# The last two output chunks: the second half stored chunk by chunk

## The chip, the cores and the metric

The kernel runs on one NeuronCore of a Trainium2 chip. The metric is the device time of one execution in microseconds (us), the median over several runs. A profiled execution of the same program gives, beside its time, a span: from the first to the last instruction on the core's engines. The engines are TensorE (PE in the profile, its weight loads PEld), VectorE (DVE), ScalarE (ACT), GpSimd (POOL) and SyncE (SP). SP, ACT and POOL each issue DMA transfers from a queue of their own (SPq, ACTq, POOLq); in the profile's DMA part, q1 carries SP's transfers, q10 ACT's and q0 POOL's.

## The reference: what is computed

The output is a sum over one array x of 2048 rows and 640 columns:

```python
xn = layernorm(x)
a, b = xn @ dft_hid_re.T, xn @ dft_hid_im.T          # along the 640 columns
fourier = dft_seq_re @ a - dft_seq_im @ b            # along the 2048 rows
mlp = gelu(xn @ w1 + b1) @ w2 + b2                   # 640 -> 1536 -> 640
out = x + fourier + mlp
```

All of it is float32. On the chip a float32 operand is split into a high and a low part, and a product is three matmuls (high-high, high-low, low-high).

## The kernel before, in words

The 2048 rows are taken in four row blocks of 512 (`NT = 4`, `TB = 512`). The first part of the kernel is the layernorm, the MLP and the products that build the transformed halves of the input; the last part, which starts long before the lines that matter here, runs the Fourier sums along the rows and then, for pairs of row blocks, the product with the hidden transform. What these leave in PSUM is transposed (the layout of the output in SBUF is 32-row bands, `B = 32`), added to the x + MLP part, and stored. The scheduling is by hand: each stage is a list of entries (`entries`), TensorE's matmuls of an entry are issued first, and `beside` or `hidden_beside` names what the other engines do behind that entry. The order in which the code names operations is the order in which they stand on each engine.

The change lies in the very last entries of the last pair. There, row block `ta` (tile `yo`, 128 partitions x 16 x 160 columns, `blocks[-2][1]`) still lacks its two last chunks of 32 columns in each 160-column quarter, columns 64 to 96 and 96 to 128, `2 * B : 4 * B`. They lie in the PSUM banks `X` and `X + 1`. In its last entries TensorE completes them in halves of 256 columns (`HALVES`), 15 matmuls each: the first half of bank `X`, the first half of bank `X + 1`, the second half of `X`, and last the second half of `X + 1`. Half `u` becomes the rows `u * 8` to `u * 8 + 8` of the 16 in `yo`. For each half:

- `turn_rows(u, j)` (L1703, its transpose is L1706) transposes half `u` of bank `X + j` on VectorE, into the scratch `rt2` or, with `dst`, straight into `yo`. For the very last one the old content of `yo` was added into the PSUM bank ahead, so that no add is left behind it.
- `add` (L462, its instruction is L463) adds the scratch into `yo`.
- `store_rows` (L1708) calls `store` (L1276, its DMA is L1280), which sends the rows to DRAM as one DMA for each of the four quarters, two from SP's queue and two from ACT's. With both chunks a run of 64 columns, 256 bytes, is contiguous; a DMA is 32 partitions x 8 rows x 256 bytes, 64 KB.

`upper_rows` does that for the first half, `lower_rows` for the second half: turn chunk 0, add it, turn chunk 1 into place, then four DMAs with both chunks. In front of them on the same queues stand the stores of the other row block of the pair (`out_dram<-u` on SP and ACT, `out_dram<-y` on POOL).

Every DMA of SP and ACT carries one of eight completion semaphores, which the framework gives out in turn in the order of issue over both queues. A DMA whose turn comes to a semaphore again waits, on its queue, until the DMA that had it before has landed. The closing code on SP (L1779) waits for the eight semaphores one after the other, in the fixed order of their numbers 0 to 7, and then all engines meet in two barriers. In the kernel before, the four DMAs of `upper_rows` have semaphores 1 and 3 (SP), 0 and 2 (ACT), and the four of `lower_rows` have 5 and 7 (SP), 4 and 6 (ACT).

Of the kernel before, what the change touches and what calls it, by code (L numbers as in the profile page):

```python
# [17 lines left out]
B = 32  # L18
# [8 lines left out]
def kernel(  # L27
# [45 lines left out]
    nc = tc.nc  # L73
# [18 lines left out]
    def pool(name, side="left", stack=ctx):  # L92
        return stack.enter_context(tc.tile_pool(name=name, bufs=1, side=side, reuse_waits="tile"))
# [22 lines left out]
    def bank(k):  # L116
        return banks[:, k]
# [19 lines left out]
    rows = pool("rows", side="right", stack=es_rows)  # L137
# [60 lines left out]
    def rows_of(ap, t):  # L198
        return ap[t * TB : (t + 1) * TB].rearrange("(n r) d -> r n d", r=B)
# [262 lines left out]
    def add(dst, a, b, op=ALU.add):  # L462
        nc.vector.tensor_tensor(dst, a, b, op=op)  # L463


    blocks = [(0, t) for t in range(NT)] + [(1, t) for t in (NT - 1, *range(NT - 1))]
# [239 lines left out]
    v, r, t = others[:, :, 1], others[:, :, 3], others[:, :, 4]  # L706
# [569 lines left out]
    def store(t, src, c0, c1, *queues, rows=slice(None)):  # L1276

        queues = queues or (nc.sync,)
        for q in range(Q):
            queues[q % len(queues)].dma_start(  # L1280
                rows_of(out, t)[:, rows, q * DQ + c0 : q * DQ + c1], src[q * B : (q + 1) * B]
            )
# [44 lines left out]
    yo = {}  # L1327
# [365 lines left out]
    def last_rows(u):  # L1693

        rows = slice(u * NB // 2, (u + 1) * NB // 2)
        return rows, yo[blocks[-2][1]][:, rows, 2 * B : 4 * B].rearrange("p n (e i) -> p e n i", i=B)

    def turned_rows(u):

        t = A["rt2"][:, 1, 0].rearrange("p a b -> p (a b)")[:, u * TB : (u + 1) * TB]  # L1700
        return t.rearrange("p (e n i) -> p e n i", e=2, i=B)

    def turn_rows(u, j, dst=None):  # L1703

        src = bank(X + j)[:, HALVES[u]].rearrange("p (n i) -> p n i", i=B)
        nc.vector.transpose(turned_rows(u)[:, j] if dst is None else dst, src)  # L1706

    def store_rows(rows):  # L1708

        t = blocks[-2][1]  # L1710
        store(t, yo[t][:, rows, 2 * B : 4 * B], 2 * B, 4 * B, nc.sync, nc.scalar, rows=rows)

    def upper_rows():

        rows, d = last_rows(0)
        add(d, d, turned_rows(0))
        store_rows(rows)

    def lower_rows():

        rows, d = last_rows(1)
        turn_rows(1, 0)
        add(d[:, 0], d[:, 0], turned_rows(1)[:, 0])
        turn_rows(1, 1, d[:, 1])
        store_rows(rows)

    first = 0
    for kind, what in stages:
# [55 lines left out]
```

## Time and profile before

| what | value |
|---|---|
| time, median of 3 runs | 850.54 us (850.37 to 850.61) |
| time of the profiled execution | 850.49 us |
| its span | 848.5 us |
| TensorE busy | 842.5 us, 99% of the span |
| VectorE busy | 687.1 us, 81% |
| ScalarE busy | 368.8 us, 43% |
| end of the last matmul | 844.44 us from the start of the span |
| end of the last VectorE instruction (L1706) | 844.92 us |

A row of the timeline has the start in us from the span's start, the duration, the engine, the line, the operation, output <- input and how many there are; a merged row covers several. The duration of a DMA row (SPq, ACTq) is the time that its queue takes to issue it, not that of the transfer; "to landing" is from the start of the issue to the last completion signal.

### The profile page before, as it was taken

How to read it: one execution, taken by the hardware profiler on the slowest of the kernel's cores; microseconds unless marked ns; L12 is line 12 of the kernel's file. 1: busy time of each engine (PE TensorE's matmuls, PEld its weight loads, DVE VectorE, ACT ScalarE, POOL GpSimd, SP SyncE). 2: the span in 40 equal slices, each digit the busy share in tenths (PEclk: the TensorE clock that was granted, in tenths of full speed). 3: DMA queues.
4: the chain of work that ended last, by engine and by line, in shares of the span. 5: the costliest groups of instructions: out<-in, count | busy, mean ns of one | idle time of the engine just before them, and what ended most of it. 6: DMA issues, size and time to landing. Idle time of an engine off the chain costs nothing.

```text
span 848.5 us, 10660 instructions
## 1 busy us (share of the span) xinstructions
PE 842.5 (99%) x3741; PEld 698.6 (82%) x3741; DVE 687.1 (81%) x912; ACT 368.8 (43%) x527; POOL 67.6 (8%) x116
## 2 busy tenths in 40 slices
PE   9999999999999999999999999999999999999998
PEld 7888888888888888888888888888888888888887
DVE  7969888767854778979979787899977998886687
ACT  7655666545453555443444343232322433223241
POOL 0440024222301000000000000000000000000002
PEclk9999999999999999999999999999999999999999
DMA  7995757878987897948744679663744799805354
GB/s 222 291 247 163 149 159 249 265 222 298 254 203 201 336 321 139 208 118 198 156 137 107 167 219 292 158 142 95 218 151 156 230 234 230 311 19 180 124 168 112
DMA packets 197094, 166.53 MB, mean 196 GB/s; under 512 B 59601, under 2 KB 168145, under 8 KB 196529
## 3 DMA queue, kind: packets, MB, share of 16 engines
q1 hardware_dynamic: 187296, 140.42, 61.8%
q0 software_dynamic: 7600, 24.91, 8.8%
q10 hardware_dynamic: 2144, 0.52, 0.3%
q8 instruction: 29, 0.48, 0.2%
q14 instruction: 25, 0.20, 0.1%
HBM read 115.75 MB, written 46.14 MB: 191 GB/s over the span
## 4 chain that ended last, share of the span: by engine, by line
PE 99%; DVE 0%; issue 0%
PE banks L301 30%; PE banks L300 30%; PE banks L302 30%; PE banks L320 10%; PE banks L666 1%; PE banks L682 0%; DVE zeros L655 0%; DVE yo L1706 0%; DVE warm L657 0%
## 5 line engine op out<-in xcount | busy, mean ns | idle before, releaser
L301 PE MATMUL banks<-as,xab 128*128 128x512 f32 (+1 forms) x417 | 160.1, 384 | 0.0
L300 PE MATMUL banks<-as,xab 128*128 128x512 f32 (+1 forms) x417 | 160.1, 384 | 0.0
L302 PE MATMUL banks<-as,xab 128*128 128x512 f32 (+1 forms) x417 | 160.1, 384 | 0.0
L186 ACT ACTIVATE as<-r 128x1024 fp32r<-128x1024 f32 x80 | 85.0, 1062 | 171.2 <-PE banks L302 147.4
L189 DVE TENSOR_TENSOR as<-r,as 128x1024 fp32r<-128x1024 f32 x80 | 97.1, 1215 | 38.1 <-ACT as L186 38.0
L301 PEld LDWEIGHTS banks<-as,xab 128*128 128x128 f32 x417 | 78.3, 188 | 15.6
L300 PEld LDWEIGHTS banks<-as,xab 128*128 128x128 f32 x417 | 78.3, 188 | 15.5
L302 PEld LDWEIGHTS banks<-as,xab 128*128 128x128 f32 x417 | 78.3, 188 | 15.4
L301 PE MATMUL banks<-as,xc 128*128 128x512 f32 x224 | 87.1, 389 | 0.0
L300 PE MATMUL banks<-as,xc 128*128 128x512 f32 x224 | 87.1, 389 | 0.0
L302 PE MATMUL banks<-as,xc 128*128 128x512 f32 x224 | 87.1, 389 | 0.0
L186 ACT ACTIVATE as<-rt 128x1024 fp32r<-128x1024 f32 x32 | 34.0, 1062 | 72.5 <-PE banks L302 57.9
L320 PE MATMUL banks<-xt,xab 128*128 128x512 f32 x240 | 56.8, 390 | 0.0
L189 DVE TENSOR_TENSOR hs<-ab,hs 128x512 fp32r<-128x512 f32 x36 | 24.7, 685 | 36.2 <-ACT hs L186 36.2
L320 PEld LDWEIGHTS banks<-xt,xab 128*128 128x128 f32 x240 | 45.0, 188 | 9.4
L301 PEld LDWEIGHTS banks<-as,xc 128*128 128x128 f32 x224 | 42.0, 188 | 8.8
L302 PEld LDWEIGHTS banks<-as,xc 128*128 128x128 f32 x224 | 42.0, 188 | 8.7
L300 PEld LDWEIGHTS banks<-as,xc 128*128 128x128 f32 x224 | 42.0, 188 | 8.7
L1280 POOL DMA_DIRECT2D out_dram<-u x4 | 2.6, 657 | 568.3 <-DVE u L463 568.3
L300 PE MATMUL banks<-hs,xc 128*128 128x512 f32 x120 | 46.7, 389 | 0.0
L301 PE MATMUL banks<-hs,xc 128*128 128x512 f32 x120 | 46.7, 389 | 0.0
L302 PE MATMUL banks<-hs,xc 128*128 128x512 f32 x120 | 46.7, 389 | 0.0
(240 smaller groups left out, 1679.8 us busy)
## 6 DMA issues: line engine op xcount, KB each, us to landing
raw<-in_A_dft_seq_re_dram SPq DMA_DIRECT2D x64, 256.0 KB, 5.4
raw<-in_A_dft_seq_im_dram SPq DMA_DIRECT2D x64, 256.0 KB, 5.1
w1r<-in_B_w_dram SPq DMA_DIRECT2D x144, 80.0 KB, 3.3
wit<-wst POOLq DMA_DIRECT2D x15, 384.0 KB, 4.3
wit<-wst POOLq DMA_DIRECT2D x20, 256.0 KB, 4.2
forms_ab<-xab SPq DMA_DIRECT2D x4, 1280.0 KB, 7.6
xab<-wit SPq DMA_DIRECT2D x13, 384.0 KB, 4.1
row<-xn SPq DMA_DIRECT2D x14, 320.0 KB, 5.3
```

The lines of the kernel that those rows point to most:

```text
L186: nc.scalar.activation(h, s, AF.Copy)
L189: nc.vector.tensor_tensor(l, s, h.bitcast(F32), op=ALU.subtract)
L300: nc.tensor.matmul(acc, wh, mh, start=first, stop=False, skip_group_check=goes_on)
L301: nc.tensor.matmul(acc, wh, ml, start=False, stop=False, skip_group_check=goes_on)
L302: nc.tensor.matmul(acc, wl, mh, start=False, stop=last, skip_group_check=goes_on)
L320: nc.tensor.matmul(acc, W1[i][:, a, j * P : (j + 1) * P], XT[j][:, b], start=n == 0, stop=n == len(steps) - 1)
L666: nc.tensor.matmul(wacc, warm[:, :P], warm, start=True, stop=True)
L1280: queues[q % len(queues)].dma_start(rows_of(out, t)[:, rows, q * DQ + c0 : q * DQ + c1], src[q * B : (q + 1) * B])
```

## The change

`store_rows` gets a range of chunks. `lower_rows` stores chunk 0 of the second half when it is added, ahead of the last transpose, and chunk 1 alone after the last transpose. Eight DMAs of 32 KB, whose contiguous runs are 128 bytes, stand where four of 64 KB with runs of 256 bytes stood. `upper_rows` is as before.

```diff
-    def store_rows(rows):
+    def store_rows(rows, j0=0, j1=2):
 
-        t = blocks[-2][1]
-        store(t, yo[t][:, rows, 2 * B : 4 * B], 2 * B, 4 * B, nc.sync, nc.scalar, rows=rows)
+        t, c0, c1 = blocks[-2][1], (2 + j0) * B, (2 + j1) * B
+        store(t, yo[t][:, rows, c0:c1], c0, c1, nc.sync, nc.scalar, rows=rows)
...
         rows, d = last_rows(1)
         turn_rows(1, 0)
         add(d[:, 0], d[:, 0], turned_rows(1)[:, 0])
+        store_rows(rows, 0, 1)
         turn_rows(1, 1, d[:, 1])
-        store_rows(rows)
+        store_rows(rows, 1, 2)
```

In the changed program the instructions of TensorE, VectorE and POOL are the same in the same order. SP and ACT have two DMAs more each. The chunk 0 DMAs take semaphores 5 and 7 (SP), 4 and 6 (ACT), and the chunk 1 DMAs come round to 1 and 3 (SP), 0 and 2 (ACT), those of the `upper_rows` DMAs.

## The prediction

> **What bounds the kernel now.** I read the page first, then the end of the timeline, then the landing of each store there, and last how full the DMA engines are.
>
> ```profile
> span 848.5 us, 10660 instructions
> PE 842.5 (99%) x3741; PEld 698.6 (82%) x3741; DVE 687.1 (81%) x912; ACT 368.8 (43%) x527; POOL 67.6 (8%) x116
> PE 99%; DVE 0%; issue 0%
> ```
>
> TensorE is the bound from start to end, and the change issues nothing ahead of its last matmuls. So only what stands behind TensorE can move. That is the end of the timeline:
>
> ```profile
> 843.16 0.43 DVE L463 TENSOR_TENSOR yo<-yo,rt 128x256 f32<-128x256 f32 x1
> ...
> 844.16 0.28 PE L302 MATMUL banks<-as,xab 128*128 128x256 f32 x1
> 844.47 0.45 DVE L1706 STREAM_TRANSPOSE yo<-banks 128x256 f32<-128x256 f32 x1 [0.89 <-PE banks L302]
> 844.95 0.81 SPq L1280 DMA_DIRECT2D out_dram<-yo  x2
> 844.96 0.88 ACTq L1280 DMA_DIRECT2D out_dram<-yo  x2
> ```
>
> Chunk 0 of the second half is added at 843.59; VectorE then waits 0.89 us for TensorE, and the last turn ends at 844.92. The four last stores are issued from 844.95 to 845.84, and the span ends at 848.5: 3.6 us after the last turn are stores, their landing and the closing. All that the change can win or lose is in them. What the closing on SP waits for:
>
> ```profile
> SPq L1280 <- DVE yo L1706: 1.7, 1, 1.7
> SPq L1779 <- DMA out_dram<-yo: 0.9, 2, 0.5
> SPq L1779 <- PEq L1779: 0.7, 2, 0.5
> SPq L1779 <- DMA out_dram<-y: 0.4, 1, 0.4
> ```
>
> The first row shows that SP's queue stood idle for 1.7 us ahead of the last stores: a place in which chunk 0 can be issued. The second shows that the closing waits for the landing of the stores. The landings, one store to a pair of rows (issue duration in ns and start; then the landing after that start), the two second stores of the upper half first, then three of the last four:
>
> ```profile
> L1280 SPq DMA_DIRECT2D out_dram<-yo x1: 453/453/453, 842.8 to 842.8; - x1
> DMA to landing us min/median/max: 2.6/2.6/2.6
> ...
> L1280 ACTq DMA_DIRECT2D out_dram<-yo x1: 483/483/483, 842.8 to 842.8; - x1
> DMA to landing us min/median/max: 2.9/2.9/2.9
> ...
> L1280 SPq DMA_DIRECT2D out_dram<-yo x1: 316/316/316, 845.0 to 845.0; - x1
> DMA to landing us min/median/max: 1.7/1.7/1.7
> ...
> L1280 SPq DMA_DIRECT2D out_dram<-yo x1: 443/443/443, 845.3 to 845.3; - x1
> DMA to landing us min/median/max: 1.9/1.9/1.9
> ...
> L1280 ACTq DMA_DIRECT2D out_dram<-yo x1: 463/463/463, 845.4 to 845.4; - x1
> DMA to landing us min/median/max: 2.1/2.1/2.1
> ```
>
> ACT's second store ends last: issued at 845.37 (845.84 less its 0.46), landed at 845.4 + 2.1 = 847.5. From there to 848.5 is the closing, 1.0 us. How full the DMA engines are (the columns: stretch, length, busy time of PE, PEld, DVE, ACT and POOL, PE clock, DMA share, GB/s):
>
> ```profile
> 818.50:819.50 1.00, 1.00 (x6) 0.84 (x5) 1.00 (x2) 0.80 (x1) 0.00 (x0) 1.00 1.35 208
> 813.00:814.00 1.00, 1.00 (x6) 0.83 (x5) 1.00 (x2) 0.51 (x1) 0.00 (x0) 1.00 0.84 200
> 843.60:844.45 0.85, 0.84 (x8) 0.63 (x6) 0.00 (x0) 0.00 (x0) 0.54 (x1) 1.00 1.12 168
> 844.45:845.45 1.00, 0.00 (x0) 0.00 (x0) 0.45 (x1) 0.00 (x0) 0.00 (x0) 1.00 1.06 253
> 845.45:845.75 0.30, 0.00 (x0) 0.00 (x0) 0.00 (x0) 0.00 (x0) 0.00 (x0) 1.00 0.11 28
> 845.75:847.10 1.35, 0.00 (x0) 0.00 (x0) 0.00 (x0) 0.00 (x0) 0.00 (x0) 1.00 0.86 194
> 847.10:848.40 1.30, 0.00 (x0) 0.00 (x0) 0.00 (x0) 0.00 (x0) 0.00 (x0) 0.77 0.00 0
> ```
>
> The engines are full to 845.45 (the upper half's second stores and POOL's `y` stores), nearly idle for 0.30 us, and carry the last four stores from 845.75 to 847.10. So data starts 845.75 - 844.95 = 0.8 us after the issue, and the landing comes 847.5 - 847.10 = 0.4 us after the last data. The first two rows price the run length: runs of 128 bytes flow at 208 GB/s (the stretch with 0.21 MB in 1585 packets, nearly all under 512 B), runs of 256 bytes at 200.
>
> ```profile
> DMA packets 1585, 0.21 MB, mean 208 GB/s; under 512 B 1581, under 2 KB 1581, under 8 KB 1585
> ...
> DMA packets 797, 0.20 MB, mean 200 GB/s; under 512 B 797, under 2 KB 797, under 8 KB 797
> ```
>
> Halving the runs therefore doubles the packets and leaves the time for the same bytes: 4 x 64 KB = 0.26 MB in 1.3 us, and half of it, 0.13 MB, in 0.63 us.
>
> **The change part by part.** The four chunk 0 stores can issue at 843.6. Two such issues take 0.81 us on SP and 0.88 on ACT (the timeline), and both queues are idle then, so they are through by 844.5, ahead of the last turn's end at 844.92. They cost nothing on the queues; without that idle stretch they would cost these 0.9 us. They wait for semaphores 4 to 7, whose last stores were those of `u`; the later one of ACT's,
>
> ```profile
> L1280 ACTq DMA_DIRECT2D out_dram<-u x1: 507/507/507, 840.1 to 840.1; - x1
> DMA to landing us min/median/max: 3.5/3.5/3.5
> ```
>
> landed at 843.6, in time. The last turn itself writes rows that lie between those being stored, but it is built with a wait for TensorE alone, so it stays at 844.47.
>
> *Term A, a new wait.* The chunk 1 stores come round to the semaphores of the upper half's stores. ACT's second one needs the upper store that landed at 842.8 + 2.9 = 845.7. It is issued at about 845.75 instead of 845.37: +0.38. Nothing of use is queued behind it on ACT; who waits is SP's closing. (SP's second one needs 842.8 + 2.6 = 845.4, about 0.1 later than now; it lands ahead of ACT's.) Bounds: 0, if that store landed early, and +0.9, if it took the 3.5 us of the `u` store above.
>
> *Term B, a shorter last transfer.* ACT's last store carries 32 KB instead of 64 and by now has nearly no neighbour. The nearest row is SP's first of the last four, 1.7 us, which also started on idle engines; half the bytes take 0.16 us less at 200 GB/s, 1.54, and its issue is one of a second store, 0.1 longer: I take 1.65. Against 2.1 that is -0.45. Bounds: no gain at all, 0; and 0.8 + 0.16 + 0.4 = 1.36 us, the three stretches above with nothing beside it, -0.74.
>
> *Term C, chunk 0's own data.* 0.13 MB take 0.63 us of the engines. They become ready around 844.4, where the engines are full, and the idle stretch takes 0.27 of them (0.89 of 0.30 us): the engines are free of them by about 845.45 + 0.36 = 845.8. ACT's last data comes at 845.75 + 0.8 = 846.55, well behind. What is left is that they mix with the upper store for which term A waits. I take +0.1; bounds 0 and the whole +0.63.
>
> *Term D, the closing.* SP takes the eight semaphores in order. Now the one that lands last is 6, with one wait (7) behind it. Then it is 2, with five behind it, each already met. What a met wait costs:
>
> ```profile
> L1779 SPq EVENT_SEMAPHORE  x2: 28/28/28, 847.5 to 847.6; - x2
> L1779 SPq DRAIN  x2: 7/7/7, 847.6 to 847.7; - x2
> ```
>
> Four instructions start within 0.2 us, some 0.06 from one to the next. Four more waits: +0.25. Bounds: 0.11 (four times 28 ns) and 0.4 (four times the 0.1 between the two in the row).
>
> Sum: 0.38 - 0.45 + 0.1 + 0.25 = +0.28 us on the profiled execution's 850.49, so 850.77; the median of the runs is 0.05 above it, which gives **850.8**. That is +0.03%; about 0.2%, 1.7 us, is what a measurement of this kernel can tell from no change.
>
> **A rule against the change.** ACT's 64 KB landed in 2.1 us where its neighbours were busy, SP's in 1.7. The Trainium skill, "DMA: Bandwidth & Descriptors", section "Anatomy of one DMA", puts a transfer issued by GpSimd at about 2.0 us plus its bytes at 436 GB/s, nearly all of it fixed; by that an estimate for 64 KB is 2.15 us and for 32 KB 2.08. Term B would be -0.07 instead of -0.45, and the sum 851.2. The rows here are of SP's and ACT's queues and go down to 1.7, so I keep the rows.
>
> **The rivals.**
>
> *The landing is fixed.* If ACT's last store takes 2.1 us whatever it carries, B is 0, and the sum is +0.73: 851.3. For it: 64 KB landed in anything between 1.7 and 2.9 us, so bytes are not what sets it. Against it: the 1.7 belongs to the store that had the engines to itself, and that is what the last one will have. Chance 0.2. It is the case of the rule above.
>
> *Chunk 0 gets in the way (slower).* The point from which it decides is whether its packets go ahead of the upper half's ACT store on the engines. Then term C is 0.63 and not 0.1, at the gate of term A: +0.81, 851.3; with no gain in B besides, +1.26, 851.8. For it: the DMA share of 1.06 from 844.45 to 845.45. Against it: on each queue the upper stores are in front. Chance 0.1. The same page, section "Queues, rings and completion order", says that a completion signal lands only behind all earlier writes of its DMA engine, across queues; no row here shows that.
>
> *The small store lands at once (faster).* B at its bound of -0.74, C at 0 and D at 0.11 give 0.38 - 0.74 + 0.11 = -0.25: 850.3. If the gate of term A were also open by 845.37, -0.63, 849.9; the 2.9 us landing speaks against that. Chance 0.15.
>
> *The last turn waits for the chunk 0 stores.* Their second ones are issued at about 844.0 and land some 2.1 us later, 846.1; the turn would start there instead of at 844.47: +1.6 in place of A, with B and D +1.4, 851.9, and 852.4 where B brings nothing. The built program has no such wait. Chance 0.02.
>
> The forecast keeps 0.53, from 850.5 to 851.1 by its middle bounds.
>
> **How the numbers follow.** The range of 850.2 to 851.5 holds the forecast, the fixed landing, the smaller half of chunk 0's price and the upper half of the small store's: about 0.85. Faster by over 0.2% would be below 848.8, further than all bounds together reach: 0.01. Slower by over 0.2% is above 852.2: half of the turn that waits, 0.01, and 0.02 for bounds of A, B and C that add up. Within 0.2%: 0.96.
>
> **What would show it.** The last turn at 844.5 as before, and four ACT and SP issues around 843.6 to 844.5. On ACT, a stretch from 845.33 to about 845.75 in which the second chunk 1 store waits for a landing (A). Its landing 1.5 to 1.8 us after its issue (B; 2.1 is the first rival). The upper half's second ACT store at 2.9 to 3.0 us (C; 3.4 and more is the second). The last landing followed by about 1.2 us instead of 1.0 to the span's end (D). I am wrong if the last turn starts late, if the gate is open by 845.4, or if SP's store and not ACT's lands last.

## The result and the profile after

The changed kernel takes 852.42 us (median of 10 runs, 851.89 to 853.44), the kernel before 850.65 in the runs beside it: 1.77 us slower, a ratio of 1.0021 with a 95% interval of 1.0011 to 1.0031. I had forecast 850.8 and a range that ended at 851.5.

The end of the timeline of the changed kernel, the wait of SP's queue from 845 us on that ends with a landing (total, number, longest), and the engines in the stretches that answer to those of the prediction:

```profile
span 850.3 us, 10666 instructions
```

```profile
843.38 0.43 DVE L463 TENSOR_TENSOR yo<-yo,rt 128x256 f32<-128x256 f32 x1
844.70 0.45 DVE L1706 STREAM_TRANSPOSE yo<-banks 128x256 f32<-128x256 f32 x1 [0.89 <-PE banks L302]
```

```profile
SPq L1780 <- DMA out_dram<-yo: 2.1, 2, 1.9
```

```profile
845.68:846.00 0.32, 0.00 (x0) 0.00 (x0) 0.00 (x0) 0.00 (x0) 0.00 (x0) 1.00 0.98 175
846.00:847.60 1.60, 0.00 (x0) 0.00 (x0) 0.00 (x0) 0.00 (x0) 0.00 (x0) 1.00 1.00 168
847.60:850.20 2.60, 0.00 (x0) 0.00 (x0) 0.00 (x0) 0.00 (x0) 0.00 (x0) 0.77 0.01 3
```

The last turn ends at 845.15 instead of 844.92, and it waits for TensorE as long as before (0.89 us). It is the whole execution that stands 0.2 us later, and nothing in the change reaches so far forward; in the profiles of the runs below, e8 apart, the last turn ends anywhere from 844.87 to 845.59, so this is scatter. What grew is the tail, from the end of the last turn to the end of the span: 850.3 - 845.15 = 5.1 us instead of 3.6. SP's closing alone waits 1.9 us for one landing. The idle stretch of the DMA engines is filled, as forecast (share 0.98 from 845.68 to 846.00, where it was 0.11), and data stops at 847.6, only 0.3 us later against the last turn than before. But then come 2.6 us without data, where there were 1.4.

The landings say why. All eight stores of the second half, chunk 0's four first, each with its issue and, under it, its landing after the start of the issue:

```profile
L1280 SPq DMA_DIRECT2D out_dram<-yo x1: 377/377/377, 843.8 to 843.8; - x1
DMA to landing us min/median/max: 2.9/2.9/2.9
...
L1280 ACTq DMA_DIRECT2D out_dram<-yo x1: 442/442/442, 843.8 to 843.8; - x1
DMA to landing us min/median/max: 3.6/3.6/3.6
...
L1280 SPq DMA_DIRECT2D out_dram<-yo x1: 478/478/478, 844.3 to 844.3; - x1
DMA to landing us min/median/max: 3.4/3.4/3.4
...
L1280 ACTq DMA_DIRECT2D out_dram<-yo x1: 478/478/478, 844.3 to 844.3; - x1
DMA to landing us min/median/max: 3.6/3.6/3.6
...
L1280 SPq DMA_DIRECT2D out_dram<-yo x1: 316/316/316, 845.2 to 845.2; - x1
DMA to landing us min/median/max: 2.9/2.9/2.9
...
L1280 ACTq DMA_DIRECT2D out_dram<-yo x1: 374/374/374, 845.2 to 845.2; - x1
DMA to landing us min/median/max: 3.1/3.1/3.1
...
L1280 SPq DMA_DIRECT2D out_dram<-yo x1: 432/432/432, 845.8 to 845.8; - x1
DMA to landing us min/median/max: 2.6/2.6/2.6
...
L1280 ACTq DMA_DIRECT2D out_dram<-yo x1: 322/322/322, 846.2 to 846.2; - x1
DMA to landing us min/median/max: 2.4/2.4/2.4
```

Adding each pair gives landings at 846.7, 847.4, 847.7, 847.9, 848.1, 848.3, 848.4 and 848.6. The first two of the last four were issued at once behind the last turn, with no gate (the wait for the landing of the DMA that had the same semaphore before, term A of the prediction), and still took 2.9 and 3.1 us, where 64 KB took 1.7 and 2.0 before. The 2.0 is ACT's first of the last four in the kernel before:

```profile
L1280 ACTq DMA_DIRECT2D out_dram<-yo x1: 375/375/375, 845.0 to 845.0; - x1
DMA to landing us min/median/max: 2.0/2.0/2.0
```

From 847.4 on there is one landing every 0.2 us, whenever it was issued: they look like a queue. It is not a queue for the transfer of the data, since the last five landings, 847.9 to 848.6, come after the data has stopped at 847.6. ACT's last store was issued at 846.18 because it waited for the second upper store of ACT, which landed at 843.0 + 3.1 = 846.1 (2.9 us after its issue before):

```profile
L1280 ACTq DMA_DIRECT2D out_dram<-yo x1: 477/477/477, 843.0 to 843.0; - x1
DMA to landing us min/median/max: 3.1/3.1/3.1
```

### The profile page after: what moved, and what is told of

The parts are those of the page before. It is cut to its first block, busy times and chain, and to the rows that moved or that the text cites. A ratio compares the mean times of both kernels' runs of the same rounds, so it can differ in the third digit from the quotient of the medians.

```text
span 850.3 us, 10666 instructions
## 1 busy us (share of the span) xinstructions
PE 841.6 (99%) x3741; PEld 697.7 (82%) x3741; DVE 686.7 (81%) x912; ACT 368.7 (43%) x527; POOL 67.6 (8%) x116
## 4 chain that ended last, share of the span: by engine, by line
PE 98%; DMA 1%; DVE 0%; ACT 0%; SPq 0%; issue 0%; ACTq 0%
PE banks L301 29%; PE banks L300 29%; PE banks L302 29%; PE banks L320 10%; DMA row<-in_A_x_dram 1%; PE banks L682 0%; DVE st L215 0%; ACT xp L714 0%; SPq L208 0%; DVE yo L1706 0%; DVE mv L216 0%; ACT mv L707 0%; DVE mv L708 0%; ACTq L707 0%
```

## The experiments

Four theories for the late landing: chunk 0's bytes fill the engines (1); runs of 128 bytes land late by themselves (2); two stores that write the two halves of the same 256 bytes hold each other up (3); completions follow each other at a fixed pace, so that more DMAs land later, whatever is in them (4). The gate and the closing come on top in each. The experiments that send something elsewhere use this helper, which stores like `store` but to an array of the same row pitch that nobody reads (`n` is the number of DMAs, four if it is not given):

```python
def spare_rows(name, rows, c0, c1, n=Q):
    t = blocks[-2][1]
    to = dram.tile([TB, D], F32, name=name)[:, :].rearrange("(n r) d -> r n d", r=B)
    for q in range(n):
        (nc.sync, nc.scalar)[q % 2].dma_start(
            to[:, rows, q * DQ + c0 : q * DQ + c1], yo[t][q * B : (q + 1) * B, rows, c0:c1])
```

Because the differences are of the size of a run's scatter, I read each run twice: the median time, and the profile's tail, split at the last landing. All are in this table; the tail is the span less the end of the last turn, and its two parts come from the records of the completion signals in the trace. Each tail is that of one profiled execution, so a difference of 0.1 us between two rows says little. The kernel before had medians of 850.65 to 850.74 beside them.

| run | tail | last landing after the last turn | closing behind it | median time |
|---|---|---|---|---|
| before | 3.55 | 2.58 | 0.97 | 850.65 |
| changed | 5.11 | 3.46 | 1.65 | 852.42 |
| e1 chunk 1 alone | 3.33 | 2.36 | 0.97 | 850.36 |
| e2 chunk 0 elsewhere | 4.96 | 3.31 | 1.65 | 852.16 |
| e3 four tiny, then both chunks | 4.79 | 3.14 | 1.65 | 852.05 |
| e4 chunk 0 elsewhere, then both chunks | 5.23 | 3.58 | 1.65 | 852.64 |
| e5 two tiny, then both chunks | 4.11 | 2.74 | 1.37 | 851.19 |
| e6 four tiny, early | 4.00 | 2.66 | 1.35 | 851.03 |
| e7 chunk 0's bytes in two DMAs | 4.56 | 3.19 | 1.37 | 851.61 |
| e8 uneven cut | 3.54 | 2.57 | 0.97 | 851.82 |
| e9 four tiny, then chunk 1 | 4.78 | 3.13 | 1.65 | 851.81 |
| e10 four tiny, early, all on ACT | 4.09 | 2.77 | 1.32 | 851.18 |
| e11 chunk 0's bytes in wide runs | 4.89 | 3.23 | 1.65 | 852.00 |

Except for e8, whose last turn itself comes later, the tail's difference to before gives the median's difference to about 0.2 us: the loss is in the tail, in profiled and unprofiled runs alike.

**e1: chunk 1 alone.** Against the changed kernel:

```diff
-        store_rows(rows, 0, 1)
```

> The changed kernel without the four chunk 0 stores: chunk 0 of the second half does not reach the output, all else is as in the changed kernel. The last stores get semaphores 4 to 7 as in the kernel before, so there is no gate and the closing is as before. Theory 1 (chunk 0's data holds up the upper half's stores and the last ones): the last store lands 1.5 to 1.8 us after its issue instead of 2.1, and the time is 850.1 to 850.4. Theory 2 (runs of 128 bytes land late whatever else is in flight): 2.4 us or more, and 850.9 or more.

It took 850.36 us, ratio 0.9993 (0.9984 to 1.0003). ACT's last store landed 1.9 us after its issue:

```profile
L1280 ACTq DMA_DIRECT2D out_dram<-yo x1: 463/463/463, 845.3 to 845.3; - x1
DMA to landing us min/median/max: 1.9/1.9/1.9
```

The time is in theory 1's range, the landing 0.1 us above it. Theory 2 falls: runs of 128 bytes with nothing else land no later than runs of 256. What halving the last bytes is worth is 0.2 us, not the 0.45 of term B.

**e2: chunk 0 elsewhere.**

```diff
-        store_rows(rows, 0, 1)
+        spare_rows("spare", rows, 2 * B, 3 * B)
```

> The changed kernel with the four chunk 0 stores sent to another DRAM array with the same row pitch, so that no two stores write the two halves of the same 256 bytes; chunk 0 of the second half does not reach the output. Theory 1: nothing changes, 852.0 to 852.8. Theory 3 (the two halves of a 256-byte piece, written by two stores in flight together, hold each other up): the last landing comes within 1.7 us of its issue and the time is 851.0 to 851.4.

852.16 us, ratio 1.0016 (1.0006 to 1.0026); the last landing comes 2.5 us after its issue. Theory 3 falls: with no shared 256-byte piece 1.4 us of the loss stay.

**e3: four tiny DMAs in chunk 0's place.** Against the kernel before:

```diff
         add(d[:, 0], d[:, 0], turned_rows(1)[:, 0])
+        spare_rows("spare", slice(8, 9), 2 * B, 3 * B)
         turn_rows(1, 1, d[:, 1])
```

> The kernel before with four tiny DMAs (32 runs of 128 bytes each, to a DRAM array that nobody reads) where the change has the chunk 0 stores. The last stores are those of the kernel before, 64 KB with runs of 256 bytes, but they come round to the upper half's semaphores: the gate and the later place in the closing, without chunk 0's data. Gate 0.35 to 0.6 us, closing 0.25 to 0.65 us: 851.2 to 851.9. If chunk 0's data is nearly all of the loss, the gate is at the low end and the time at most 851.2.

852.05 us, ratio 1.0015 (1.0005 to 1.0024): 1.3 us of the loss are there with 16 KB in place of chunk 0's 128. That is above what I had given to gate and closing together, and the landing shows why, since it is 0.56 us later. Theory 1 can be at most the rest. The first two and the last of the last four stores, as in the list above:

```profile
L1280 SPq DMA_DIRECT2D out_dram<-yo x1: 334/334/334, 845.1 to 845.1; - x1
DMA to landing us min/median/max: 2.6/2.6/2.6
...
L1280 ACTq DMA_DIRECT2D out_dram<-yo x1: 376/376/376, 845.1 to 845.1; - x1
DMA to landing us min/median/max: 2.8/2.8/2.8
...
L1280 ACTq DMA_DIRECT2D out_dram<-yo x1: 341/341/341, 846.1 to 846.1; - x1
DMA to landing us min/median/max: 2.1/2.1/2.1
```

The first two have no gate and are the stores of the kernel before, which landed in 1.7 and 2.0 us; behind four tiny DMAs it is 2.6 and 2.8. This led to theory 4.

**e4: chunk 0 elsewhere, both chunks last.**

```diff
-        store_rows(rows, 0, 1)
+        spare_rows("spare", rows, 2 * B, 3 * B)
         turn_rows(1, 1, d[:, 1])
-        store_rows(rows, 1, 2)
+        store_rows(rows)
```

> The changed kernel with chunk 0's stores sent to another DRAM array, and as its last stores the four of the kernel before, both chunks in runs of 256 bytes. The gate, the closing and chunk 0's data as in the changed kernel, the last stores with twice the bytes in as many runs. Theory 1: the landing is at least as late as in the changed kernel, 852.3 to 853.0. Theory 2: the landing goes back to 2.1 us after the issue, 851.8 to 852.1.

852.64 us, ratio 1.0022 (1.0012 to 1.0031), in theory 1's range; the last landing comes 3.58 us after the last turn against e2's 3.31. Twice the bytes in the last stores cost 0.3 us; wide runs give nothing back. Against e3, which has the same last stores behind four tiny DMAs, chunk 0's bytes cost 0.44 us of landing (3.58 less 3.14).

**e5: two tiny DMAs.** As e3, with one on SP and one on ACT:

```diff
+        spare_rows("spare", slice(8, 9), 2 * B, 3 * B, 2)
```

> The kernel before with two tiny DMAs (32 runs of 128 bytes, one on SP, one on ACT, to a DRAM array that nobody reads) where the change has four. The last four stores come to semaphores 7, 6, 1 and 0, whose DMAs have landed before the last turn ends: no gate, and almost no data. Theory 4 (completion signals follow one another on the DMA engines no faster than about 0.18 us each, across all queues and whatever the bytes): SP's first last store lands 2.1 to 2.3 us after its issue instead of 1.7, the last landing comes about 0.2 us later than before, and with the closing the time is 851.4 to 851.8. Theory 1, or a gate alone: landings as in the kernel before (1.7 and 2.1), and only the closing is longer: 851.0 to 851.4.

851.19 us, ratio 1.0004 (0.9995 to 1.0014). By the time it is the other theories' number; by the landings it is theory 4, as the first and the last of the last four show:

```profile
L1280 SPq DMA_DIRECT2D out_dram<-yo x1: 328/328/328, 845.1 to 845.1; - x1
DMA to landing us min/median/max: 2.1/2.1/2.1
...
L1280 ACTq DMA_DIRECT2D out_dram<-yo x1: 497/497/497, 845.5 to 845.5; - x1
DMA to landing us min/median/max: 2.3/2.3/2.3
```

No store waits for a gate here, and SP's first takes 2.1 us, between 1.7 (none added) and 2.6 (four added): 0.4 to 0.5 us for every two DMAs of 4 KB. The last landing moves less at first, 2.58, 2.74 and 3.14 us for none, two and four, because in the kernel before the stores come far enough apart. Where they queue they land 0.18 us apart, the last four of e3 at 2.60, 2.79, 2.96 and 3.14. Two more such steps on e5's 2.74 give 3.10, and e3 has 3.14: it has a gate and e5 has none, so by this working the gate adds next to nothing to what the queue costs. It is not tested by itself, for no run has four added DMAs near the end and no gate. e3's last store alone could be told the other way: it was issued 0.61 us later than before and took 2.1 us as before, which makes up the whole 0.56. What speaks for the queue are the stores without a gate: e3's first two land 0.86 and 0.73 us later after the last turn than in the kernel before.

**e6: four tiny DMAs early.** Against the kernel before, in `hidden_beside`:

```diff
-            16: [] if last else [load_yb(1)],
+            16: [lambda: spare_rows("spare", slice(0, 1), 0, B)] if last else [load_yb(1)],
```

> The kernel before with four tiny DMAs issued three entries earlier, ahead of the other block's stores, so that the semaphores go round by four: the last stores get 0 to 3, whose earlier DMAs landed long ago. No gate, no more completions near the end, only the place in the closing differs. Landings as in the kernel before, and the closing longer: by 0.25 us if it is four met waits alone (850.9 to 851.1), by 0.6 if the longer way from SP's drain to the barrier that the changed kernel shows belongs to it (851.2 to 851.5).

851.03 us, ratio 1.0004 (0.9994 to 1.0013), where I had put the met waits alone. The landings are back (2.66 against 2.58) and the closing is 0.38 longer. In its trace the met waits of term D take 0.28 us more from the last landing to SP's first drain. The other 0.1 comes from a pause: one instruction of SP's closing starts 0.37 us behind the end of the one before it, where 0.07 is usual. Most of it is covered here, since at that place SP waits for the other engines anyway, 0.45 us in the kernel before. In the changed kernel the pause stands two instructions earlier, ahead of that wait, and all of it counts.

**e7: chunk 0's bytes in two DMAs.**

```diff
-        store_rows(rows, 0, 1)
+        spare_rows("spare", slice(0, 16), 2 * B, 3 * B, 2)
```

> The changed kernel with chunk 0's place taken by two DMAs of 64 KB (16 rows in runs of 128 bytes, one on SP, one on ACT, to another DRAM array): all of chunk 0's bytes and runs, half of its completions, and no gate. Chunk 0 of the second half does not reach the output. Theory 4: the last landing comes 2.2 to 2.4 us after its issue, as with two tiny ones, 851.2 to 851.6. Theory 1 (bytes): 2.6 us or more, 851.8 to 852.3.

851.61 us, ratio 1.0009 (0.9999 to 1.0018). The time is at the edge of theory 4's, the landing of ACT's last store, 2.7 us after its issue, is theory 1's. So bytes count too: against e5, with as many DMAs, chunk 0's 128 KB put the last landing 0.45 us later, and halving the last stores' bytes is already taken off in that. There is no gate here, and the last four land 0.15 to 0.17 us apart all the same.

**e8: uneven cut.** Against the kernel before:

```diff
-    HALVES = (slice(0, TB // 2), slice(TB // 2, TB))
+    CUT = 3 * TB // 4
+    HALVES = (slice(0, CUT), slice(CUT, TB))
...
-        rows = slice(u * NB // 2, (u + 1) * NB // 2)
+        rows = slice(HALVES[u].start // B, HALVES[u].stop // B)
...
-        t = A["rt2"][:, 1, 0].rearrange("p a b -> p (a b)")[:, u * TB : (u + 1) * TB]
+        t = A["rt2"][:, 1, 0].rearrange("p a b -> p (a b)")[:, 2 * HALVES[u].start : 2 * HALVES[u].stop]
```

> The kernel before with its last two chunks cut at three quarters instead of half: the upper part has 12 of 16 rows and matmuls of 384 columns, the lower part 4 rows and matmuls of 128 columns. As many DMAs as before, the last four with 32 KB each in runs of 256 bytes, and a last turn of 128 columns. The last bytes get fewer, as the change wanted, and the completions do not get more. Theory 4: a shorter last turn (0.3 instead of 0.45 us) and last stores that land 1.7 to 1.9 us after their issue: 850.2 to 850.6. If the short matmuls cost more than that brings: 850.7 to 851.2.

851.82 us, ratio 1.0013 (1.0004 to 1.0023), above both ranges: no better version. Its tail is that of the kernel before, and ACT's last store lands 2.1 us after its issue, not in the 1.7 to 1.9 that I gave. So a quarter instead of a half brought nothing behind the last turn, though the upper half's stores are larger here and may be in the way. And TensorE ends later. Two matmuls in a row of its last 30, and the last turn:

```profile
843.27 0.27 PE L300 MATMUL banks<-as,xab 128*128 128x128 f32 x1
843.38 0.28 PE L301 MATMUL banks<-as,xab 128*128 128x128 f32 x1
```

```profile
845.82 0.32 DVE L1707 STREAM_TRANSPOSE yo<-banks 128x128 f32<-128x128 f32 x1 [1.03 <-PE banks L302]
```

A matmul of 128 columns starts 0.11 us after the last; one of 256 took 0.12 (844.04 to 844.16 in the timeline before). Half the columns save next to nothing, while the upper part's matmuls of 384 columns start 0.17 us apart: with 30 of each, 30 x 0.05 - 30 x 0.01 = 1.2 us more. The last turn starts 1.35 us later.

**e9: four tiny, then chunk 1.**

```diff
-        store_rows(rows, 0, 1)
+        spare_rows("spare", slice(8, 9), 2 * B, 3 * B)
```

> The changed kernel with each of its four chunk 0 stores cut to one row (32 runs of 128 bytes, to another DRAM array): as many DMAs, gate and closing as in the changed kernel, one eighth of chunk 0's bytes. Chunk 0 of the second half does not reach the output. Theory 4 (completions set the landing): the last landing comes 3.1 us after the last turn's end, as with four tiny DMAs ahead of the full last stores, and halving the last stores' bytes brings nothing: 851.9 to 852.2. If bytes set it: 2.7 to 2.9 us and 851.5 to 851.8.

851.81 us, ratio 1.0013 (1.0004 to 1.0023): just under what theory 4 gave and at the edge of what bytes gave. The landing decides, 3.13 us after the last turn's end, theory 4's number. Beside e3 this is the plainest pair: the last stores carry half the bytes, and the last landing stays (3.13 and 3.14). Where completions set the landing, what the change gained in bytes is gone. The last store, issued behind its gate:

```profile
L1280 ACTq DMA_DIRECT2D out_dram<-yo x1: 340/340/340, 846.5 to 846.5; - x1
DMA to landing us min/median/max: 2.2/2.2/2.2
```

Beside the changed kernel it prices chunk 0's bytes: 0.33 us of landing (3.46 less 3.13), 0.6 us in the medians.

**e10: the early tiny ones all on ACT.** As e6, with `nc.scalar` for all four.

> The kernel before with four tiny DMAs three entries earlier, as in the run with them on both queues, but all four on ACT: the semaphores go round by four, and SP has no instruction more than in the kernel before. If the pause of about 0.3 us in the closing stands at a fixed place of SP's own instruction stream (theory 5), it is hidden again: the closing, from the last landing to the end, is 1.2 to 1.3 us, and the time 850.8 to 851.0. If the pause comes with the order of the semaphores: 1.35 us or more.

851.18 us, ratio 1.0005 (0.9995 to 1.0015): above the range that I gave, and the closing, 1.32 us, is just over it. The rows of the closing tell more than the sum. First the drains of the changed kernel, then those of this one (the duration's smallest, median and largest in ns):

```profile
L1780 SPq DRAIN  x3: 7/7/131, 849.0 to 849.7; - x3
L1780 ACTq DRAIN  x2: 8/79/150, 846.5 to 849.7; - x2
```

```profile
L1788 SPq DRAIN  x3: 7/7/7, 848.2 to 848.5; - x3
L1788 ACTq DRAIN  x2: 135/143/151, 846.0 to 848.8; - x2
```

SP's long drain is gone, and ACT has one where it had 8 ns: the pause has moved to the queue that got the instructions, and the barrier waits for it there. Counted in the traces, SP's pause stands ahead of the 848th instruction that the trace records on SP in every run that has more than 848 (849 in e6, 850 in e5 and e7, 851 in the others and in the changed kernel). The kernel before has exactly 848; its last one waits for the barrier at that place, so that a pause there would not show. So the place seems to belong to the engine's own instruction stream; on ACT this rests on the one run. What the pause is was not settled.

**e11: chunk 0's bytes in wide runs.**

```diff
-        store_rows(rows, 0, 1)
+        spare_rows("spare", slice(8, 12), B, 3 * B)
```

> The changed kernel with chunk 0's four stores replaced by four of the same 32 KB each in runs of 256 bytes (4 rows, 64 columns, to another DRAM array): the same bytes, completions, gate and closing, half the runs. Chunk 0 of the second half does not reach the output. If the short runs cost, the last landing goes from 3.3 or 3.5 us after the last turn's end to 3.1 to 3.2 and the time is 851.9 to 852.1. If bytes or completions alone count: 3.3 to 3.5 us and 852.1 to 852.4.

852.00 us, ratio 1.0015 (1.0005 to 1.0024), last landing 3.23 against e2's 3.31. The time lies where I had put "short runs cost", the landing between the two; with 0.08 us of difference I take the length of the runs to be worth nothing that this can tell.

## Why the prediction was wrong

The forecast was +0.28 us on the profiled execution, and the tail grew by 1.56. In the order of its steps:

- **What bounds the kernel, and that the change acts behind the last turn alone:** right. TensorE and the last turn keep their order and their wait of 0.89 us; the tail has 1.56 of the 1.78 us by which the span grew, and the rest is the scatter ahead of it.
- **Chunk 0 is issued beside TensorE's last matmuls:** right. Its issues start at 843.8, 0.03 us behind the add that ends at 843.81, and cost the queues nothing.
- **Term A, the gate:** there, and larger: ACT's last store is issued 1.03 us after the last turn's end instead of 0.45 (846.18 and 845.15), because the upper half's store now lands 3.1 us after its issue. It was counted as a cost in the sum. By the working under e5 it is covered, since the landing is queued anyway; no run takes the gate away alone.
- **Term B, the shorter last transfer, is the step that failed, and the largest part of the miss.** I took 1.65 us from the one store that had landed in 1.7, and argued that ACT's last one "by now has nearly no neighbour". It has nine: when it is issued, POOL's last two, chunk 0's four and its own three are all still to land. It took 2.4 us: +0.3 instead of -0.45. With four 4 KB DMAs in chunk 0's place (e9) it is 2.2, without them (e1) 1.9: even alone the shorter transfer is worth 0.2, not 0.45.
- **Term C, chunk 0's data:** priced as time of the engines, 0.63 us less what the idle stretch takes, and so +0.1 on the upper store for which term A waits; that store landed 0.2 us later. The price that I left out is that of the four DMAs themselves, which delay every later landing. Four of 4 KB each move the last landing by 0.56 us (e3) or, with chunk 1 alone behind them, by 0.76 (3.13 in e9 against 2.36 in e1), the gate included; chunk 0's bytes add 0.33 to 0.44 (e9 and e4).
- **Term D, the closing:** 0.68 instead of 0.25. The met waits are 0.28 of it, as forecast; 0.4 is the pause in SP's stream, which nothing in the trace of the kernel before shows.
- **The sum in the prediction's terms:** A and C 0.58 (issue at 1.03 instead of 0.45; forecast 0.48), B +0.29 (-0.45), D 0.68 (0.25), together 1.55. Of the 1.28 us that the forecast missed, 0.74 are B, 0.43 are D and 0.1 are A and C.
- **The sum as the runs split it:** 0.56 for four more completions and their gate, 0.32 for chunk 0's bytes less the halving (3.46 less e3's 3.14), 0.28 and 0.4 for the closing: together the 1.56 us by which the tail grew.
- **The rivals:** chunk 0 getting in the way came nearest, with the wrong price; its upper end of 851.8 lacks the pause. The turn that waits for the stores did not happen.

The prediction also read the price of short runs wrongly. Its row of 208 GB/s for runs of 128 bytes is not from stores but from loads of `xab`, the only DMAs in that stretch (line, size and time to landing):

```profile
xab<-wit SPq DMA_DIRECT2D x2, 384.0 KB, 3.9
```

And the DMA share in that row is 1.35 against 0.84 for runs of 256 bytes, so byte for byte the engines were busy about 1.5 times as long; in the changed kernel the stretch from 846.0 to 847.6, mostly short runs, moved 168 GB/s at a share of 1.00. This did not decide the case: e11, with half as many runs in chunk 0, lands 0.08 us before e2.

The rule that I set against the trace, a transfer issued by GpSimd is nearly all fixed time (the Trainium skill, "DMA: Bandwidth & Descriptors", section "Anatomy of one DMA"), gave 851.2 and was a little nearer than my rows. Its direction, that the bytes of a last store buy little, is what e1 and e9 show. The sentence that I left beside the second rival, that a completion lands only behind all earlier writes of its engine, across queues (the Trainium skill, "DMA: Bandwidth & Descriptors", section "Queues, rings and completion order"), fits the runs: DMAs of 4 KB from SP and ACT take 2.8 to 3.3 us behind the stores of POOL and of the upper half. No run here shows the mechanism itself, only the queue of landings.

## What to carry to other kernels

At the end of a kernel count the DMAs still to land as well as their bytes: here two more of 4 KB cost 0.16 us of the last landing and four more 0.56 to 0.76, 128 KB ahead of the last stores cost 0.33 to 0.45, and halving the last transfer gained 0.2 once. Splitting a last store so that half of it can go early adds completions ahead of the ones that matter. It could pay if the early ones landed before the last are issued; here they took 2.9 to 3.6 us, and no run tries it with the real data (e6 does with four DMAs of 4 KB, and the landing is nearly that of before). And read from the program which semaphore each last DMA comes round to and where the closing waits for it.

## What the runs showed that I had not expected

- Behind one another the landings of SP's and ACT's stores come 0.15 to 0.2 us apart at the end, and in no trace closer, for 4 KB as for 64 KB. POOL's landings do not keep to it: in e2, e4 and e7 one falls within 0.06 us of ACT's. The Trainium skill ("DMA: Bandwidth & Descriptors", section "Anatomy of one DMA") says that the semaphore write itself is almost free; these landings differ from that, if it is what they wait for, which no run shows.
- The pause of 0.3 to 0.4 us at a fixed place of an engine's instruction stream: hidden in the kernel before, and exposed by three more instructions on SP (the changed kernel) or moved to ACT (e10).
- Matmuls of 128 columns start 0.11 us apart here (e8), those of 256 columns 0.12 apart (the kernel before).
